# A fused convolution and gated feed-forward kernel: early loads reordered, four x loads put behind the first transposes, fill convolutions moved late

One core of one Trainium2 chip. The metric is the device time of one execution in microseconds (us); "the clock" is the TensorE clock that the throttle granted, as a share of full speed. 1 KB below is 1024 bytes as the profile prints it; MB are 10^6 bytes.

## The reference

```python
# x: (8, 4096, 192) f32; weight: (8 heads, 7 taps); w_in: (192, 2048); w_out: (2048, 192)
w = softmax(weight, axis=-1)                      # per head
c[b, s, h*24:(h+1)*24] = sum_k w[h, k] * x[b, s - 6 + k, h*24:(h+1)*24]   # causal, zero-padded
h = c.reshape(32768, 192) @ w_in
out = (h * cos(h)) @ w_out
```

## The kernel before

A convolution is a set of TensorE matmuls with a banded matrix, in blocks of 112 tokens. Its result stands with tokens on partitions; the feed-forward part wants channels there, so it is transposed. The first two convolutions (convs 0 and 1, blocks 0 to 4) are transposed on TensorE; all later ones by DMA. A token tile has 512 tokens. For each, 16 up-projections ("U", six matmuls of 512 columns each), 16 cosines on ScalarE ("S"), 16 multiplies on VectorE ("M"), and 32 down-projections ("d", two sets of 16) are interleaved by strings of letters. Before the steady strings comes a fill in which inputs arrive: "k" in it runs the next job of a list (mostly a cast on GpSimd). In the steady strings "p" casts the x of a later conv and loads ahead, and "x" and "y" store results.

The first token tile needs blocks 0 to 4. The second, from U16 on, needs blocks 4 to 9, thus convs 2, 3 and 4, which are the three 64-channel chunks of blocks 5 to 12, and one DMA transpose of each.

```python
def load_blocks(b, k0, n, queues=(nc.sync, nc.sync)):      # two DMAs of 384 KB for n = 4
    ...
# pairs: what one conv covers; loads: groups of up to 4 blocks: 0-3, 4, 5-8, 9-12, 13-14, 15-18, 19-22, ...
load_blocks(*loads[0], (nc.sync, nc.scalar)); load_blocks(*loads[1])
...
load_w1(0); load_w1(1)                                     # w_in in four chunks of 768 KB
state = {"conv": 0, "loaded": 2, "cast": 2}

def load_ahead(n=2, queues=(nc.sync, nc.sync)):            # what the next n conv casts need
    last = max(pairs[min(state["cast"] + n, NC) - 1])[:2]
    while last not in xws:
        load_blocks(*loads[state["loaded"]], queues)
        state["loaded"] += 1

load_ahead(1, (nc.sync, nc.scalar))                        # blocks 5 to 12, for convs 2, 3, 4
...
load_w1(2); load_w1(3); load_w2(0); load_w2(1)             # w_out in two halves
...
def conv_out(p, ps):
    ct = evacuate(p, ps)                                   # PSUM to SBUF on ScalarE
    ...
        nc.sync.dma_start_transpose(out=dst, in_=ct[0:rows, j:j + m]...)   # same queue as the loads
...
    elif op == "p":
        cast_pair(); load_ahead()
...
def later():                                               # the jobs behind "k"
    yield from (lambda q=q: cast_w1(1, q) for q in range(NCH))
    yield cast_pair                                        # conv 2's x
    yield lambda: load_ahead(4)                            # blocks 13-14, 15-18, 19-22
    yield from (lambda q=q: cast_w1(2, q) for q in range(NCH))
    yield cast_pair
    yield cast_pair
    yield from (lambda q=q: cast_w1(3, q) for q in range(NCH))
    yield from (lambda c=c, q=q: cast_w2(c, q) for c in range(2) for q in range(4))

fill("kkkkkUSMUSMUSMkkkUSMUSMkkkUSMCceUSMkkUSMCceUSMkkkkkkkkUSMCceUSMUSMU")   # C, c: a conv; e: evacuate, transpose
for k in range(NSETS - 2):
    emit("dddSMdUdMSUdSdMUdSMd" + ("p" if k == 0 else "") + "UdMSUdSdMCcdedMUdpSdUyxUMS")
```

Three times in each set of downs the two halves of the array swap PSUM banks; a tiny memset on GpSimd, the "mark", carries that order. It stands in GpSimd's program order with the casts.

## Time and profile before

| | |
|---|---|
| time, median of 3 | 730.85 us (730.48 to 731.51) |
| TensorE busy | 709.4 of 730.0 us |
| TensorE busy from 50 to 700 us | 100% |
| U16, first tile-2 up-projection: due / start / end | 37.96 / 41.96 / 43.97 us |

TensorE sets the end, and is short of work in the first 50 us only. There the 16 DMA engines are the busy part. So the start has to be read as a queue: which bytes stand ahead of which on the one issuing queue, and what waits for them. The lines are in the prediction below.

### The profile page before, as it was taken

Reading aid. Unit: us, or ns where it says so; the run is one execution under the profiler, and the core shown is the slowest. Engines: PE = TensorE matmul, PEld = TensorE weight load, DVE = VectorE, ACT = ScalarE, POOL = GpSimd, SP = SyncE. Lnnn points to the kernel's source line nnn. Section 1 sums busy time; section 2 is a strip of 40 time slices with the busy share of each in tenths; the row PEclk is TensorE's granted clock in tenths of the full one; section 3 lists DMA queues with packets and bytes.
Section 4 is the critical chain, followed back from the end, with each engine's and each line's share of the span. In section 5 each row is a group of like instructions: output and inputs, shape, how many; then the busy total and the mean of one; then the engine's idle time right before and its main releaser. Section 6 shows DMA issues by size and latency. Waiting matters only on the chain.

```text
span 730.0 us, 27515 instructions
## 1 busy us (share of the span) xinstructions
PE 709.4 (97%) x12284; PEld 528.2 (72%) x12284; DVE 641.9 (88%) x594; ACT 589.0 (81%) x641; POOL 95.4 (13%) x345
## 2 busy tenths in 40 slices
PE   6779999999999999999999999999999999999997
PEld 4457777777777777777777777777777777777776
DVE  6659989999989989989989988989989999999994
ACT  4758888888888888888888888888888888787773
POOL 3601011011011011011011111111111110000000
PEclk9889999999999999999999999999999999999999
DMA  9956251644546266262655445526172331011101
GB/s 217 276 74 145 60 131 46 139 95 117 113 93 132 61 120 129 61 157 50 144 98 128 82 90 119 144 71 150 44 157 59 98 71 55 24 45 46 45 25 66
DMA packets 126339, 72.58 MB, mean 99 GB/s; under 512 B 52428, under 2 KB 124684, under 8 KB 126220
## 3 DMA queue, kind: packets, MB, share of 16 engines
q1 hardware_dynamic: 124330, 69.44, 41.5%
q8 instruction: 96, 1.57, 0.9%
q10 hardware_dynamic: 1890, 1.37, 0.8%
q14 instruction: 23, 0.19, 0.1%
HBM read 33.48 MB, written 25.17 MB: 80 GB/s over the span
## 4 chain that ended last, share of the span: by engine, by line
PE 94%; DMA 4%; DVE 0%; ACT 0%; POOL 0%; issue 0%; SPq 0%; ACTq 0%; POOLq 0%
PE h L286 48%; PE acc L286 46%; DMA xw<-in_moe_w_out_dram 1%; DMA xw<-in_moe_w_in_dram 1%; DMA xw<-in_x_dram 1%; DMA cT<-ct 1%; DVE g L396 0%; ACT cos L391 0%; POOL w L245 0%; SPq L371 0%; ACTq L80 0%; POOL w L235 0%; DVE osb L433 0%; ACT osb L433 0%; SPq L232 0%
## 5 line engine op out<-in xcount | busy, mean ns | idle before, releaser
L396 DVE TENSOR_TENSOR g<-h,cos 128x1024 bf16<-128x1024 f32 x512 | 604.2, 1220 | 36.8 <-ACT cos L391 30.0
L391 ACT ACTIVATE cos<-h 128x1024 bf16<-128x1024 f32 x512 | 511.2, 1024 | 113.9 <-PE h L286 95.4
L286 PEld LDWEIGHTS <-g 64*128 64x128 bf16 x8192 | 354.4, 94 | 102.4 <-POOL mark L296 2.9
L286 PE MATMUL h<-cT,w 64*128 64x512 bf16 x3072 | 409.9, 378 | 8.1 <-DMA cT<-ct 4.0
L286 PE MATMUL acc<-w,g 64*128 64x192 bf16 x8064 | 416.8, 243 | 0.4 <-POOL mark L296 0.3
L286 PEld LDWEIGHTS <-w 64*128 64x128 bf16 x3072 | 149.1, 94 | 85.2 <-issue 5.3
L296 POOL MEMSET mark<- 1x1 f32 x192 | 17.1, 89 | 610.7 <-PE acc L286 602.1
L433 DVE COPY osb<-acc 128x384 f32<-128x384 f32 x63 | 35.1, 558 | 40.4 <-PE acc L286 40.4
L161 POOL CAST xb<-xw 128x512 bf16<-128x512 f32 (+1 forms) x113 | 64.9, 606 | 9.1 <-DMA xw<-in_x_dram 7.9
L344 ACT CAST ct<-h 112x1024 bf16<-112x1024 f32 (+2 forms) x53 | 52.5, 990 | 9.5 <-PE h L286 5.9
L286 PEld LDWEIGHTS <-band 64*128 64x128 bf16 x952 | 31.6, 96 | 5.3 <-issue 4.9
L433 ACT COPY osb<-acc 128x384 f32<-128x384 f32 x63 | 29.8, 473 | 5.7 <-PE acc L286 5.7
L286 PE MATMUL h<-xb,band 64*128 64x192 bf16 (+10 forms) x912 | 34.2, 214 | 0.0
L235 POOL CAST w<-xw 128x512 bf16<-128x512 f32 x12 | 7.0, 616 | 7.0 <-DMA xw<-in_moe_w_in_dram 7.0
L286 PE MATMUL h<-w,g 64*128 64x192 bf16 x128 | 5.9, 243 | 0.3 <-POOL mark L296 0.3
L183 PE MATMUL acc<-unit 128*112 128x112 bf16 x46 | 4.8, 302 | 1.3 <-POOL unit L166 1.3
L286 PE MATMUL acc<-xb,band 64*128 64x192 bf16 (+2 forms) x40 | 2.4, 264 | 3.7 <-POOL xb L161 3.7
L342 ACT CAST ct<-acc 112x512 bf16<-112x512 f32 x6 | 3.2, 599 | 3.0 <-PE acc L286 2.9
L183 PEld LDWEIGHTS <-unit 128*112 128x112 bf16 x46 | 4.4, 211 | 1.4 <-POOL unit L166 1.3
L245 POOL CAST w<-xw 128x384 bf16<-128x384 f32 x8 | 3.7, 510 | 1.6 <-DMA xw<-in_moe_w_out_dram 1.6
L196 ACT ACT_TABLE_LOAD x1 | 1.3, 1283 | 2.6 <-issue 2.6
L433 DVE COPY osb<-h 128x384 f32<-128x384 f32 x1 | 0.6, 558 | 2.4 <-ACT osb L433 2.4
(37 smaller groups left out, 18.3 us busy)
## 6 DMA issues: line engine op xcount, KB each, us to landing
out_dram<-osb SPq DMA_DIRECT2D x63, 384.0 KB, 3.1
xw<-in_x_dram SPq DMA_DIRECT2D x60, 384.0 KB, 6.8
xw<-in_x_dram SPq DMA_DIRECT2D x7, 336.0 KB, 3.9
xw<-in_moe_w_in_dram SPq DMA_DIRECT2D x4, 512.0 KB, 7.0
xw<-in_moe_w_out_dram SPq DMA_DIRECT2D x2, 768.0 KB, 8.9
cT<-ct SPq DMA_TRANSPOSE x66, 2.7
xw<-in_moe_w_in_dram SPq DMA_DIRECT2D x8, 128.0 KB, 8.4
xw<-in_x_dram ACTq DMA_DIRECT2D x2, 384.0 KB, 10.5
```

What stands on the lines that cost most here:

```text
L161: copies[j % len(copies)](out=xbs[p][:, s0:s1], in_=src)
L183: nc.tensor.matmul(out=acc[0][0:W, 0:W], lhsT=unit, rhs=unit, start=True, stop=True)
L196: nc.scalar.activation(out=wex, in_=wq, func=AF.Exp)
L235: copy(out=w1[:, q, c * CW:(c + 1) * CW], in_=staged[1, c][:, q, :])
L245: nc.gpsimd.tensor_copy(out=w2[:, c * n:(c + 1) * n, :][:, fs, :], in_=staged[2, c][:, fs, :])
L286: ins = nc.tensor.matmul(out=o, lhsT=w, rhs=r, start=start, stop=stop, skip_group_check=True)
L296: ins = nc.gpsimd.memset(mark, 0.0)
L342: copy(out=ct[0:W, 0:n, s, :], in_=bank[0:W, 0:n * L].rearrange("p (j c) -> p j c", c=L))
L344: copy(out=ct[0:W, 0:n].rearrange("p j s c -> p s j c"), in_=ps[0:W, :, 0:n * L].rearrange("p s (j c) -> p s j c", c=L))
L391: nc.scalar.activation(out=cos, in_=hs[n], func=AF.Sin, bias=math.pi / 2.0, scale=1.0)
L396: nc.vector.tensor_tensor(out=g, in0=hs.pop(n), in1=cs.pop(n), op=ALU.mult)
L433: copy(out=osbs[k][:, 2 * bank:2 * bank + 2, :].rearrange("p a d -> p (a d)"), in_=src[:, 0:2 * D])
```

## The change

The intent: bring w_in's third chunk ahead of the x blocks for convs 2 to 4, so that up-projections run while x is on its way; run the fill's convs later, each with its evacuation right behind it; and take fewer x loads ahead of the first DMA transposes.

```diff
-    load_ahead(1, (nc.sync, nc.scalar))
+    load_w1(2)
+    load_ahead(1)
     cast(0, ...); cast(1, ...)
-    load_w1(2)
     load_w1(3)
@@ def later():
-        yield from (lambda q=q: cast_w1(1, q) for q in range(NCH))
+        yield from (lambda c=c, q=q: cast_w1(c, q) for c in range(1, 3) for q in range(NCH))
         yield cast_pair
-        yield lambda: load_ahead(4)
-        yield from (lambda q=q: cast_w1(2, q) for q in range(NCH))
+        yield lambda: load_ahead(3)
         yield cast_pair
         yield cast_pair
@@
-    fill("kkkkkUSMUSMUSMkkkUSMUSMkkkUSMCceUSMkkUSMCceUSMkkkkkkkkUSMCceUSMUSMU")
+    fill("kkkUSMUSMUSMkkkUSMUSMUSMkkUSMUSMCceUSMkkkkkCceUSMUSMkkkkkkkkCceUSMU")
```

Part A below is the order of the early loads, part B the order of casts and convs, part C `load_ahead(3)` for `load_ahead(4)`: with 3, blocks 15 to 22 (four DMAs of 384 KB) are loaded by the first "p" of the steady strings, which comes after the three transposes on the queue.

## The prediction

> **What bounds the kernel now.** I read the page's slices first, then stretches of the first 54 us, then the chain of work that ended last, then the timelines of TensorE and of the DMA-issuing engine. The slices divide the run in two:
>
> ```profile
> PE   6779999999999999999999999999999999999997
> ...
> PEclk9889999999999999999999999999999999999999
> DMA  9956251644546266262655445526172331011101
> ```
>
> One slice is 18.25 us. From the fourth on TensorE is full; in the first two the DMA engines are. The stretches agree (last columns: granted clock, DMA share, GB/s):
>
> ```profile
> 20.00:22.00 2.00, 0.00 (x0) 0.00 (x0) 2.00 (x2) 0.84 (x1) 0.62 (x1) 0.54 1.06 263
> ...
> 38.00:40.00 2.00, 0.00 (x0) 0.00 (x0) 1.55 (x2) 0.37 (x1) 0.00 (x0) 1.00 0.85 140
> ...
> 44.00:46.00 2.00, 2.00 (x19) 1.25 (x17) 0.94 (x1) 1.10 (x2) 0.09 (x1) 0.50 0.00 0
> ...
> 100.00:200.00 100.00, 100.00 (x1755) 78.01 (x1752) 91.31 (x84) 84.77 (x92) 12.65 (x48) 1.00 0.43 102
> ```
>
> TensorE is 100% busy from 50 us to past 700; there DVE has 91 of 100 us. So a microsecond that the start loses is a microsecond at the end, and this diff touches only the start. TensorE's two long waits in it:
>
> ```profile
> 22.73 1.03 PE L286 MATMUL acc<-xb,band 64*128 64x192 bf16 x12 [3.21 <-POOL xb L161]
> ...
> 37.14 0.82 PE L286 MATMUL acc<-w,g 64*128 64x192 bf16 x16
> 41.96 2.01 PE L286 MATMUL h<-cT,w 64*128 64x512 bf16 x6 [3.99 <-DMA cT<-ct]
> ```
>
> Bracketed: idle time before, and who ended it. The first waits for x blocks 5 to 12 (conv number 2); the second is the seventeenth up-projection, U16, the first on the second token tile, which needs the transposes of convs 2, 3 and 4. That second wait is on the chain of work that ended last; its links there:
>
> ```profile
> 38.38 0.71 SPq L371
> ...
> 39.14 0.02 SPq L371
> ...
> 39.18 4.13 DMA cT<-ct
> ...
> 43.36 0.61 PE h L286 x2
> ```
>
> The third transpose is issued at 39.18 and lands at 43.31; U16's last chunk follows. Why so late, when its conv was evacuated at 31.4 (ScalarE's timeline: 30.27, 1.10 us)? The issuing engine's queue, from the timeline in three windows:
>
> ```profile
> 28.00 4.77 SPq L110 DMA_DIRECT2D xw<-in_x_dram  x4
> 32.86 4.16 SPq L371 DMA_TRANSPOSE cT<-ct  x1
> 37.12 4.21 SPq L371 DMA_TRANSPOSE cT<-ct  x2
> ```
>
> Six x loads (two halves each of blocks 13-14, 15-18 and 19-22) stand ahead of the transposes on this queue, and the DMA share is full until 38.
>
> **What the Trainium skill says.** (1) "DMA: Bandwidth & Descriptors", "Queues, rings and completion order": each engine consumes a ring's descriptors in ring order. So a transpose queued behind x loads waits for their data; the trace agrees, the first transpose landing 9.1 us after its issue and a later one, on idle queues, in 3.8. (2) The same page, "Issuing engines are not separate DMA queues": work started by ScalarE and SyncE shares 16 engines. So taking half of the early x loads off ScalarE frees no bandwidth; it only changes the order. (3) "TensorE: Matmul & The Clock Gate", "What's actually happening": about 3.4 us idle halves the clock, about 3.4 us busy restores it. Agreed: after 4.0 us idle the clock is 0.50 and six 512-column matmuls take 1.51 us where they take 0.83 later. (4) "Perfetto Trace Analysis", "DMA Instruction — HWDGE (DVE, Sync)": the profiled issue ends when descriptors are generated, not when data lands. Hence I use landings.
>
> **The change part by part.** The instruction order of the two builds confirms equal work: the same 24,570 TensorE rows, two DMA starts moved from ScalarE to SyncE. No instruction of the steady part moves.
>
> *Part A, the third w_in chunk ahead of x for conv 2.* Adding the bytes of the 2-us stretches: 2.50 MB by 12 us, 3.45 by 16, 3.90 by 18, 4.86 by 22, 5.47 by 24, 7.47 by 30, 9.31 by 38. A w_in chunk is 512+128+128 KB = 0.79 MB, a four-block x load 0.79. First x loads 0.98, two chunks: 2.55 MB. Now two ScalarE halves of x (0.79 MB) compete with the second chunk, whose casts wait until 16.00 and 17.38. Without them 2.55 MB is moved by 12.2 us; with the 1 to 2 us lag seen from data to cast, the second chunk is there at about 14, the third (3.34 MB at 15.5) at 17. x for conv 2 is complete at 4.91 MB: 22.2 us, plus 2 to 2.5, cast ends about 25, against 22.68 now. So conv 2 starts near 25.1, 2.4 us later, but two more up-projections stand before it (eight, not six). They are paced by DVE's multiply, 1.18 us apart from 14.25: number 8 ends about 23.7. TensorE idles about as long as now and is cold about as long.
>
> *Part B, convs late.* After conv 2: evacuation 1.1 us, U8 cold 1.3, its cos and multiply to 29.7; now the ninth multiply ends at 30.7. Conv 3 follows at 27.3 (two casts of 0.6 behind conv 2's), conv 4 at 29.5, whose evacuation stands behind two cos: 31.5 to 32.6, against 31.37 now. The w_out bytes keep their place in the queue (7.27 MB in either order), so the downs start about 32.4 (now 32.58) and the casts of the second half of w_out gate the fourth changeover mark near 34.7, as now. **So TensorE reaches U16 at about 37.5 to 38, as now (37.96).** Part B alone is worth about nothing.
>
> *Part C, four x loads behind the transposes.* Each is 384 KB, 1.57 MB together. At the 230 to 250 GB/s of 30 to 38 us that is 6.3 to 6.8 us of queue; I take 6.4. DMA data ahead of the transposes ends at 38 - 6.4 = 31.6. The third transpose lands at 43.3 - 6.4 = 36.9, or, from its operand (32.6) plus an issue and the 4.1 us of its landing now, 36.8. Both are before TensorE comes for it, with a microsecond to spare.
>
> *The sum.* U16 ends at 43.97 now; then at 38.0 + 0.65 = 38.65: -5.3 us. The cold stretch behind it goes: from 43.36 to 48.27 TensorE does work that in the warm periods takes 0.22+0.33+1.28+0.66+0.62+0.66 = 3.77 us: -1.15. Against it, DVE used the pause to empty its queue; without it U17 and U18 wait for multiplies 14 and 15, about +0.5. Net -5.9 us: 730.85 - 5.9 = **725.0 us** (-0.8%).
>
> **The rivals.** *The transposes stay the bound.* If their issue is slow for its own sake (1.97 us for the second, on queues emptying), or w_out lands later because transposes share the engines, U16 waits until 40: gain 3 us, 728. For it: 4.16 us for the first one's issue. Against: later issues take 1.2 to 1.4 us. *A late x moves the loss, not removes it.* Conv 2 at 27 rather than 25 delays everything behind it: gain 2 to 4 us, 727 to 729. For it: TensorE already idles for just this x. Against: the lag I used is the larger one seen. *The loads put behind come too late.* They now move from about 37 to 44 and land near 45. GpSimd casts conv 6's x then (48.70 now, so about 42.7), and in-order behind it stands a changeover mark due at 52.50 - 6.2 = 46.3. Casts end near 45.6: under 1 us to spare, and 1 to 2 us lost if it fails: 726 to 727. *More gained*: if early w_in lets DVE never starve before 24 us and x is on time, everything runs 2 us ahead: 723. A gain over 2% needs 14.6 us; all TensorE idle from 12 to 42 us (1.1+0.3+1.0+3.2+0.4+0.9+0.3+4.0 and small ones, about 11.5) and the cold penalties (some 4) would have to go together. A loss of 2% has no mechanism: nothing is added.
>
> **Range and chances.** The centre is the net sum. The rivals make 723 to 729; two of the slow ones can add up, so the range is 722.3 to 728.5. Faster by over 2%: 0.01. Slower by over 2%: 0.01. Within: 0.98.
>
> **What would show it.** In the profile after: the wait of 3.99 us on a transposed chunk at U16 gone or under 1 us; U16 near 38; the third transpose landing near 37; granted clock 1.00 through 36 to 50; SyncE issuing three transposes ahead of four x loads; the second w_in chunk's casts from about 14; conv 2 near 25 behind a wait like now's; the 10.9-us periods unchanged from 50 on. The prediction is wrong if U16 still waits for a transpose until 40, if conv 2 starts at 27 or later or already at 22, if GpSimd's mark waits behind conv 6's cast, or if the steady periods change.

## The result, and the profile after

724.04 us, median of 4 runs (723.21 to 725.39), beside 730.70 us (4 runs) before: ratio 0.9909, 95% interval 0.9891 to 0.9926. A ratio here is the mean time of one kernel's fast runs over the mean of the other's fast runs of the same rounds, so not quite the ratio of the medians quoted. All runs were fast runs, and the outputs right.

The page's slices of the kernel after (busy tenths of TensorE and clock; TensorE is full from the third slice on, which ends at 54 us, and before from the fourth; in the first two it is busy for 70 to 79% of the time, and the DMA engines are as busy as before):

```profile
PE   7799999999999999999999999999999999999997
...
PEclk9999999999999999999999999999999999999999
DMA  9956333552827337254653554516273321011102
```

Stretches after, columns as before (busy us of TensorE, its weight load, DVE, ScalarE, GpSimd, each with the number of instructions; then clock, DMA share, GB/s):

```profile
38.00:40.00 2.00, 2.00 (x58) 1.62 (x54) 1.92 (x3) 1.72 (x2) 0.09 (x1) 1.00 1.13 228
...
44.00:46.00 2.00, 2.00 (x42) 1.58 (x38) 1.97 (x3) 1.32 (x3) 0.70 (x2) 1.00 0.26 48
...
100.00:200.00 100.00, 100.00 (x1742) 77.12 (x1740) 91.12 (x83) 84.82 (x92) 12.51 (x47) 1.00 0.48 104
```

Where TensorE was idle from 38 to 40 us, or at half clock at 44, it now works at full clock. The steady part is unchanged. TensorE's timeline after, the instructions that answer to the two long waits (each line starts with its start and its length in us):

```profile
25.44 0.62 PE L286 MATMUL acc<-xb,band 64*128 64x192 bf16 x12 [3.43 <-POOL xb L161]
...
36.76 0.84 PE L286 MATMUL acc<-w,g 64*128 64x192 bf16 x16
37.41 0.83 PE L286 MATMUL h<-cT,w 64*128 64x512 bf16 x6
```

The wait for x at conv 2 is as long as ever (3.43 us; 3.21 before). U16 follows the downs with no idle time. The queue of the issuing engine, SyncE, says why:

```profile
27.33 6.34 SPq L371 DMA_TRANSPOSE cT<-ct  x3
33.76 2.66 SPq L110 DMA_DIRECT2D xw<-in_x_dram  x4
```

The evacuation that the third transpose waits for, from ScalarE's timeline, and its issue, from SyncE's in a narrower window:

```profile
31.35 1.07 ACT L342 CAST ct<-acc 112x512 bf16<-112x512 f32 x2
...
32.45 1.22 SPq L371 DMA_TRANSPOSE cT<-ct  x1
```

The third transpose is issued at 32.45 us, right behind that evacuation, and its record of landing says 2.7 us: it is there at 35.1, 2.3 us before TensorE asks. Before it was issued at 39.18 and took 4.13.

The stretch from U16 to U18 shows the rest. Before (the lines of U17 and the next downs at half clock, and of U18):

```profile
44.38 1.51 PE L286 MATMUL h<-cT,w 64*128 64x512 bf16 x6
45.66 1.51 PE L286 MATMUL acc<-w,g 64*128 64x192 bf16 x16
...
48.27 0.83 PE L286 MATMUL h<-cT,w 64*128 64x512 bf16 x6
```

and after:

```profile
38.39 0.83 PE L286 MATMUL h<-cT,w 64*128 64x512 bf16 x6
39.04 0.84 PE L286 MATMUL acc<-w,g 64*128 64x192 bf16 x16
...
40.86 0.83 PE L286 MATMUL h<-cT,w 64*128 64x512 bf16 x6
```

U18 starts 48.27 - 40.86 = 7.41 us earlier, and the span is 730.0 - 722.6 = 7.4 us shorter: nothing is lost or won after it. (The profiled run of before, 731.82 us, was one of its longer ones; hence 7.4 here and 6.7 between the medians.)

### The profile page after: what moved, and what is told of

Its sections match the earlier page's. It is cut to its first block, busy times and chain, and to the rows that moved or that the text cites. A ratio compares the mean times of both kernels' runs of the same rounds, so it can differ in the third digit from the quotient of the medians.

```text
span 722.6 us, 27515 instructions
## 1 busy us (share of the span) xinstructions
PE 708.5 (98%) x12284; PEld 527.0 (73%) x12284; DVE 641.3 (89%) x594; ACT 589.1 (82%) x641; POOL 95.0 (13%) x345
## 3 DMA queue, kind: packets, MB, share of 16 engines
q8 instruction: 96, 1.57, 0.9%
## 4 chain that ended last, share of the span: by engine, by line
PE 96%; DMA 3%; SPq 1%; DVE 0%; ACT 0%; issue 0%; POOL 0%; POOLq 0%
PE h L286 49%; PE acc L286 46%; DMA xw<-in_x_dram 2%; DMA xw<-in_moe_w_in_dram 1%; SPq L110 0%; DVE g L396 0%; SPq L232 0%; ACT cos L391 0%; POOL xb L161 0%; SPq L230 0%; DVE osb L433 0%; ACT osb L433 0%; SPq L104 0%; POOLq L542 0%; POOL mark L296 0%
## 5 line engine op out<-in xcount | busy, mean ns | idle before, releaser
L433 DVE COPY osb<-acc 128x384 f32<-128x384 f32 x63 | 35.1, 558 | 39.6 <-PE acc L286 39.6
```

Of the source, the lines that this page charges most:

```text
L433: copy(out=osbs[k][:, 2 * bank:2 * bank + 2, :].rearrange("p a d -> p (a d)"), in_=src[:, 0:2 * D])
```

## The experiments

Every run was correct and all its timed runs were in the fast state. Ratios are to the kernel before in the same call. Three calls ran on three chips; the kernel before had medians of 731.78 (35 runs), 731.36 (27) and 731.50 us (27) in them.

| run | what | median us | ratio, 95% interval |
|---|---|---|---|
| call 1: e1_c_undone | A and B, not C | 730.77 | 0.9991 (0.9980 to 1.0002) |
| e2_c_alone | C | 724.25 | 0.9899 (0.9884 to 0.9915) |
| e3_a_alone | A | 730.49 | 0.9989 (0.9978 to 1.0000) |
| e4_b_alone | B | 731.34 | 0.9990 (0.9980 to 1.0000) |
| call 2: e5_one_group | the change, two of C's four loads back | 727.22 | 0.9941 (0.9929 to 0.9953) |
| e6_warm | before, TensorE kept busy 2 us of the wait | 730.92 | 0.9994 (0.9986 to 1.0002) |
| e7_later_convs | the change, conv 2 later still | 724.19 | 0.9901 (0.9888 to 0.9913) |
| e8_w2_later | and w_out casts behind a mark | 723.58 | 0.9892 (0.9879 to 0.9905) |
| call 3: c_after | the change | 724.00 | 0.9894 (0.9881 to 0.9907) |
| e9_warm_longer | before, TensorE kept busy all the wait | 730.07 | 0.9982 (0.9974 to 0.9990) |
| e10_mark_first | e8, and one cast behind the next mark | 721.85 | 0.9880 (0.9861 to 0.9899) |
| e11_a_and_c | A and C, not B | 726.33 | 0.9930 (0.9918 to 0.9942) |

### Which part is the gain: e1_c_undone, e2_c_alone, e3_a_alone, e4_b_alone

e1 is the changed kernel with one number back:

```diff
-        yield lambda: load_ahead(3)
+        yield lambda: load_ahead(4)
```

> The changed kernel with the four x loads (blocks 15 to 22) put back ahead of the transposes: parts A and B without part C. Theory (C is the whole gain): the bytes ahead of the transposes are those of the kernel before, so the third transpose lands near 42 and U16 waits some 4 us again, with the half clock behind it; time within 1.5 us of the kernel before (729 to 731). Rival (the gain comes from the third w_in chunk and the later convs keeping VectorE busy): 725 to 727.

Measured 730.77 us, 0.9991. The third transpose landed at 44.4 us, later than the 42 expected, and TensorE's timeline has the wait again:

```profile
43.13 1.95 PE L286 MATMUL h<-cT,w 64*128 64x512 bf16 x6 [4.05 <-DMA cT<-ct]
```

e2 is the kernel before with the opposite edit, `load_ahead(3)` for `load_ahead(4)`, and nothing else.

> The kernel before with the four x loads moved behind the transposes, nothing else: part C alone. Theory: third transpose lands near 36 to 37, no wait at U16 (near 38), whole gain or nearly: 723.5 to 726. Rival (A and B needed): at least half of the gain missing, 727.5 or more.

Measured 724.25 us, 0.9899: the whole gain. The third transpose landed at 35.1 us (issued at 32.1, 3.0 us), a little before the 36 to 37 expected, and U16 starts at 36.74 us without a wait, in e2's timelines of TensorE and of SyncE:

```profile
36.74 0.83 PE L286 MATMUL h<-cT,w 64*128 64x512 bf16 x6
```

```profile
27.24 6.08 SPq L371 DMA_TRANSPOSE cT<-ct  x3
33.40 2.65 SPq L110 DMA_DIRECT2D xw<-in_x_dram  x4
```

e3 is the kernel before with the early loads of the change:

```diff
-    load_ahead(1, (nc.sync, nc.scalar))
+    load_w1(2)
+    load_ahead(1)
```

(and `load_w1(2)` taken out further down).

> The kernel before with only the early loads reordered (third w_in chunk before x for conv 2, both x halves on the same queue): part A alone. Theory: conv 2 starts near 25 instead of 22.7 and there are only six up-projections before it, so TensorE idles longer there, but the wait at U16 shrinks by as much, as the bytes ahead of the transposes are unchanged: 729.5 to 732. Rival (early w_in is worth something by itself): under 728.

e4 is the kernel before with the change's `later()` and fill string, but `load_ahead(4)` and the old load order.

> The kernel before with only the order of casts, convs and evacuations of the change (convs late), loads in the old order and all x loads ahead of the transposes: part B alone. Theory: the transposes still land at about 43, so 729.5 to 732. Rival (convs late worth something): under 728.

Measured 730.49 (0.9989) and 731.34 (0.9990): both 0.1% under the kernel before, their intervals touching 1. Each part makes conv 2 wait longer (5.29 us in e3, 5.05 in e4), and nothing comes of it, since the transposes land late anyway. e3's timeline of TensorE (conv 2, then U16 in two pieces):

```profile
24.43 1.04 PE L286 MATMUL acc<-xb,band 64*128 64x192 bf16 x12 [5.29 <-POOL xb L161]
...
39.53 0.39 PE L286 MATMUL h<-cT,w 64*128 64x512 bf16 x2 [0.38 <-DMA cT<-ct]
41.84 1.21 PE L286 MATMUL h<-cT,w 64*128 64x512 bf16 x4 [1.92 <-DMA cT<-ct]
```

What follows: C is sufficient and necessary for the gain. It does not need A and B, and these without C give nothing measurable.

### What A and B do once the wait is gone: e11_a_and_c

e3 with `load_ahead(3)`.

> Parts A and C without B: loads as in the changed kernel, casts and convs in the old order, so only six up-projections stand before conv 2, which starts at 24.4 as in the run of A alone. Theory (A alone costs about 1.5 to 2 us of TensorE's arrival at U16, which the wait for the transposes hid, and B gives it back): 1 to 2.5 us over the changed kernel. Rival (A and B each nothing even without that wait): equal to the changed kernel.

Measured 726.33 us, 0.9930; c_after in the same call 724.00, 0.9894: 2.3 us slower, intervals apart. Conv 2 waits 5.57 us here:

```profile
24.39 1.04 PE L286 MATMUL acc<-xb,band 64*128 64x192 bf16 x12 [5.57 <-POOL xb L161]
...
38.75 0.83 PE L286 MATMUL h<-cT,w 64*128 64x512 bf16 x6
```

The second line is U16: 38.75 us, where C alone (e2) has 36.74 and the changed kernel 37.41. So A costs some 2 us: x comes later, while only six up-projections stand before conv 2. B, with eight, gives the 2 us back. Together they are worth nothing that these runs resolve: C alone has 0.9899, all three 0.9909 and 0.9894.

### Half the dose: e5_one_group

```diff
-        yield lambda: load_ahead(3)
+        yield lambda: (load_ahead(3), load_blocks(*loads[state["loaded"]]), state.update(loaded=state["loaded"] + 1))
```

> The changed kernel with one of the two groups of x loads (blocks 15 to 18, 0.79 MB) put back ahead of the transposes: half the dose. Theory (queue bytes ahead of the transposes set their landing, with about 2 us of slack now): landing about 3.2 us later, near 38.5, TensorE comes for it near 37.4, so a wait of about 1 us at U16 and no half clock: 0.5 to 2 us over the changed kernel. Rival (the order itself, not the bytes, costs): 3 us and more over it.

Measured 727.22 us, 0.9941. Against the changed kernel's 0.9909 and 0.9894 (other calls) that is 0.0032 to 0.0047 of 731 us, 2.3 to 3.4 us: more than I expected, and up to where the rival began (3 us), so the time alone does not refute it. TensorE's timeline:

```profile
36.31 0.79 PE L286 MATMUL h<-cT,w 64*128 64x512 bf16 x4
39.16 0.39 PE L286 MATMUL h<-cT,w 64*128 64x512 bf16 x2 [2.07 <-DMA cT<-ct]
```

The last chunk came at 39.16, where I had reckoned 38.5, and TensorE was a microsecond earlier at U16 in this run, so it waited 2.07 us and not 1. And the half clock came behind that wait (0.62 over 40 to 42 us, 0.52 over 42 to 44), which I had ruled out. What speaks for the theory is the order of the landings: with none, one and two groups of loads ahead, the third transpose landed at 35.1 (the changed kernel, where its evacuation sets its issue), 39.1 and 44.4 us (e1, by its chain of work that ended last: 40.23 plus 4.20). But both steps, 4.0 and 5.3 us, are larger than the 3.2 us that I had reckoned from the bytes of one group. A part of that is the issue itself: with x loads ahead the first transpose took 4.2 us (e5) and 4.4 us (e1) to issue, in the kernel after 2.3. So bytes ahead delay the landing, and their time is a lower bound here. Whether the same loads issued from another engine would cost as much was not run.

### What the half clock is worth: e6_warm, e9_warm_longer

```diff
         h = h_pool.tile([128, 2, T], FP32, name="h")
+        if n == 16:
+            for _ in range(36):          # 86 in e9
+                nc.tensor.matmul(out=h[0:W, 0, 0:W], lhsT=unit, rhs=unit, start=True, stop=True)
```

This is the kernel before, and U16 overwrites what these matmuls leave.

> The kernel before with 36 throw-away 112-column matmuls (about 0.1 us each) in U16's output tile just ahead of U16, to keep TensorE busy while it waits for the transposes. The result stays right. Theory (the gain of the change is the wait itself, about 5.7 us, plus about 1.7 us of half clock behind it): only the half clock goes, so 1 to 2 us under the kernel before, granted clock 1.00 after 42 us. Rival (the half clock is the larger part): 4 us or more under it. Second rival (the half clock costs nothing, as other engines set the pace there): no change.

Measured 730.92 us, 0.9994, no change, but this run decides nothing: each throw-away matmul took 57 ns, not the 0.1 us that I had taken from those at the start, so they ended at 40.7 us, TensorE idled 1.84 us more, and the clock was 0.50 from 44 to 46 us all the same. With enough of them:

> The throw-away matmuls ahead of U16 again, now 86 of them (57 ns each as measured, 4.9 us), since the 36 ended 2 to 3 us before the transposes had landed and the clock fell all the same. Theory: the granted clock stays 1.00 from 42 to 50 and the half clock's share of about 1.7 us is saved: 1 to 2 us under the kernel before. Rival (the half clock was no loss): no change, or more if the dummies end after the landing.

Measured 730.07 us, 0.9982 (0.9974 to 0.9990): 0.0018 of 731.5, 1.3 us less than the kernel before (0.7 to 1.9 by the interval). In e9's timeline U16 follows the dummies directly, at full clock:

```profile
37.62 4.65 PE L386 MATMUL h<-unit 128*112 128x112 bf16 x86
42.21 0.82 PE L286 MATMUL h<-cT,w 64*128 64x512 bf16 x6
```

and the clock from 42 to 50 us is 1.00 in its stretches. So of the gain, one to two microseconds are the half clock, and the rest is the wait.

### What bounds the start now: e7_later_convs, e8_w2_later, e10_mark_first, c_after

VectorE still has a gap of 3.73 us at 24.5 us in the changed kernel, for want of x. e7 puts two more up-projections before conv 2:

```diff
-    fill("kkkUSMUSMUSMkkkUSMUSMUSMkkUSMUSMCceUSMkkkkkCceUSMUSMkkkkkkkkCceUSMU")
+    fill("kkkUSMUSMUSMkkkUSMUSMUSMkkUSMUSMUSMUSMCcekkkkkCceUSMkkkkkkkkCceUSMU")
```

> The changed kernel with conv 2 one more pair of up-projections later (ten instead of eight before it), so that VectorE has work while x is on its way. Theory: VectorE's idle 3.7 us before the ninth multiply shrinks to 1 us or so; the start of the downs then waits for the w_out casts, so 0.5 to 2 us under the changed kernel. Rival (transposes then bind again, as their issue cannot come earlier): no change.

Measured 724.19 us: no difference that these runs resolve, where I expected 0.5 to 2 us; and not for the rival's reason, as U16 starts at 36.69 without a wait for a transpose. Conv 2 now waits 1.02 us, and TensorE is ready for the fifth down at 32.79, 1.7 us earlier than in the changed kernel (34.47), but is held for 0.94 us there by a mark which stands behind the last w_out casts on GpSimd. The next set's mark, behind conv 6's cast, costs another 0.26 us. e8 therefore moves those four casts behind that mark (four "k" fewer in the fill; the remaining jobs run in the first steady string after "dddSMdUd").

> As the previous one, and the last four w_out casts moved behind the first changeover mark on GpSimd, so that the first five downs need not wait for them. Theory: up to 1 us more than the previous one, until U16 meets the landing of the third transpose near 35 to 36: 1 to 3 us under the changed kernel. Rival: no difference from the previous one.

Measured 723.58 us, 0.9892: 0.6 us under e7, inside the intervals, and short of the 1 to 3 us that I expected under the changed kernel. U16 starts at 35.27, 2.1 us ahead of the changed kernel's 37.41, and the third rival of the prediction takes a part of it. GpSimd's timeline in e8, then TensorE's:

```profile
43.36 0.61 POOL L161 CAST xb<-xw 128x512 bf16<-128x512 f32 x1 [3.55 <-DMA xw<-in_x_dram]
43.91 0.09 POOL L296 MEMSET mark<- 1x1 f32 x1
```

```profile
44.06 0.50 PE L286 MATMUL acc<-w,g 64*128 64x192 bf16 x8 [0.55 <-POOL mark L296]
```

The loads that C put behind the transposes are waited for by conv 6's cast, and the mark stands behind it. e10 moves that cast behind the mark:

```diff
-        emit("dddSMdUd")
+        emit("dddSMd" + ("p" if k == 1 else "") + "Ud")
...
-        emit("... UdMSUdSdMCcdedMUdpSdUyxUMS")
+        emit("... UdMSUdSdMCcdedMUd" + ("p" if k else "") + "SdUyxUMS")
```

> As the run with the w_out casts behind the mark, and conv 6's x cast behind the next changeover mark as well, since in that run it held GpSimd until 43.9 and a mark behind it came 0.55 us late. Theory: that wait goes and the 2.1 us by which TensorE was ahead at 42 us are kept: 1.5 to 3 us under the changed kernel. Rival: the lead is lost elsewhere, no difference.

> The changed kernel unaltered, to have it on the same chip and beside the same runs of the kernel before as the three others of this call: ratio 0.99 again.

Measured 721.85 us (0.9880) for e10, 724.00 (0.9894) for c_after. The wait at the mark is gone from e10's timeline. Four of its five runs (721.68 to 722.40) lie below all four of c_after (722.97 to 724.24), the fifth at 725.23 above them; the intervals overlap. The median is 2.15 us lower, as expected, but the gain is not clear of the noise. Nor is all of it this edit's: in the profiled runs e10 was 0.45 us ahead of e8 at U16 already (34.82 against 35.27), before the edit acts, with a clock of 1.00 over 26 to 28 us where e8 had 0.50. If a faster version is wanted, this is the one to try further.

## Why the prediction was right

The time (725.0 foretold, 724.04 measured) and the way to it held. By its steps:

- **What bounds.** Only the start matters: U18's 7.41 us are the span's 7.4 us. Shown. (That the work is equal, the pages show with 12,284 matmuls each; the 24,570 rows of the prediction stand in no view here.)
- **Part A.** Second w_in casts from 12.71 (about 14 foretold), third from 17.19 (17), conv 2's cast done at 25.39 (25), conv 2 at 25.44 (25.1), its wait as long as before. Right. No run tried the move of the two x halves from ScalarE to SyncE by itself.
- **Part B.** First downs at 32.50 (32.4), U16 at 37.41 (37.5 to 38). "Part B alone is worth about nothing" held for the time in e4. What I did not see is that A by itself costs 2.3 us once the transposes are on time, and that B pays for it (e11): I had added their effects in one sum and not asked for each alone.
- **Part C.** The landing of the third transpose was foretold for 36.8 to 36.9, and is 35.1: with no x loads ahead it took 2.7 us from its issue, not the 4.1 of before, which the prediction had kept. The slack is 2.3 us instead of one. That all of the gain is here: shown by e1 and e2.
- **The sum.** U16's end: -5.3 foretold, 38.24 - 43.97 = -5.73 measured, as U16 ended 0.4 us earlier than the 38.65 reckoned. The half clock: -1.15 foretold. From U16's end to U18, the chains give 4.48 us before and 2.80 after, so -1.68 measured. The term was mis-sized by a slip: among the "warm" lengths I put 1.28 us for six 512-column matmuls, which was their half-clock length; warm it is 0.65. (The 0.62 for conv 5's matmuls was too long as well; after, the chain has 0.50.) e9 has -1.3 by itself. VectorE's backlog: +0.5 foretold, none measured: U17 and U18 follow the downs before them at once. The three errors all lie on the same side, so none was made good by another. Together -5.9 foretold, -7.4 in the profile, -6.7 between the medians.
- **The clock.** It is 1.00 from 36 to 50 us, as foretold. But the prediction's "agreed", for a fall after about 3.4 us of idleness, goes beyond the trace: 0.50 after the 4.0 us wait is there, yet the fall itself came sooner (last section).
- **The rivals.** The transposes did not stay the bound, and x was not later than reckoned. The third, conv 6's cast held by late loads, came within a hair: its second half was cast at 44.35 to 44.96, and the mark behind it ran at 45.09, on the pace of the others (52.50 - 7.41), so it cost nothing here. In e7 it cost 0.26 us, and in e8, two microseconds ahead, 0.55 us. GpSimd's lines after:

```profile
44.35 0.61 POOL L161 CAST xb<-xw 128x512 bf16<-128x512 f32 x1 [2.45 <-DMA xw<-in_x_dram]
45.09 0.09 POOL L296 MEMSET mark<- 1x1 f32 x1
```

Open: how much of the run-to-run spread is the clock's, and why x loads move fewer bytes per microsecond than w_out loads. By their place in the queue, w_out moves in the stretch from 26 to 30 us of the kernel before, at 362 and 368 GB/s, and x from 30 to 36 us, at 230 to 241. Both come in rows of 768 B, but each x DMA fills 64 partitions and each w_out DMA 128; no run here tells whether that is the cause.

Open too: in the kernel after, the first 18 up-projection matmuls took 3.68 us under a recorded clock of 1.00 (12 to 16 us); in c_after, the same kernel, 2.12 us. The recorded clock alone does not tell their speed:

```profile
12.67 3.68 PE L286 MATMUL h<-cT,w 64*128 64x512 bf16 x18 [0.15 <-ACT cT L490]
```

## What to carry to other kernels

On a shared DMA queue, look for prefetches issued ahead of a small transfer that everything waits for: here 1.57 MB of them, 6.4 us by their bytes, made the last transpose land 8.2 us later (43.3 against 35.1). Count the bytes that stand before it, and put what is needed later behind it. When a change has several parts, run each alone: here one number carried the gain, and two larger edits cancelled each other. A wait that is long enough hides the cost of edits made before it; that cost appears when the wait is removed.

## What the Trainium skill lacked or had wrong

- "TensorE: Matmul & The Clock Gate", "What's actually happening": it gives about 3.4 us of idleness for the fall to half clock. In these runs the length of an idle stretch does not tell whether the clock falls. In the kernel before it fell about 0.6 us after TensorE went idle at 19.52 us, and about 2.7 us after it did so at 37.97 (estimates from one-microsecond means: 1.00 over 19 to 20 us, 0.58 over 20 to 21, 0.50 after; 1.00 over 39 to 40, 0.82 over 40 to 41, 0.50 after). In e8 no idle stretch from 12 to 26 us was longer than 0.79 us, and the clock was 0.78 over 25 to 26 us and 0.50 over 26 to 27, while a stretch of 1.02 us in e7 left it at 1.00. In the kernel after it stayed at 1.00 through 3.43 us of idleness and was 0.55 in the microsecond from 26 us, after work had begun again. So a plan should not count on 3.4 us. In e8:

```profile
24.30 0.62 PE L286 MATMUL acc<-xb,band 64*128 64x192 bf16 x12 [0.79 <-POOL xb L161]
...
26.00:28.00 2.00, 1.94 (x21) 1.28 (x22) 0.03 (x1) 0.93 (x3) 2.00 (x4) 0.50 1.09 372
```

- No page has the length of the issue of a DMA transpose on this chip with other transfers ahead of it. For the same shape, the three early ones took 4.16, 1.97 and 2.15 us in the kernel before, with x loads queued ahead of the first, and 2.27, 2.28 and 1.22 us in the kernel after. The second of these took 2.28 us although the DMA engines were nearly idle in its last microsecond (share 0.15 from 31 to 32 us), so busy engines alone do not explain the length.
